# Attention with decay counted within chunks, its products pinned in groups of one tiling, and a weight's two halves added on VectorE

## The chip, the cores and the metric

The kernel runs on one core of a Trainium2 chip. The metric is the time of one execution in microseconds on the device, as the median of a few runs. Five engines work side by side, each on its own queue: TensorE (PE, with its weight loads shown as PEld), VectorE (DVE), ScalarE (ACT), GpSimd (POOL) and SyncE (SP), which issues the transfers here.

## What is computed

Three steps, in float32, on 4 batches of 8 heads with 576 places and 64 columns a head:

```python
scores = q @ k.T / sqrt(64)
D = where(rel >= 0, gamma[h] ** rel, 0)       # rel = query place - key place
x = (scores * D) @ v                          # 2304 tokens x 512
h = x @ w_in                                  # 512 -> 2048
x2 = (h * clip(h + 3, 0, 6) / 6) @ w_out      # 2048 -> 512
h2 = x2 @ w_in2                               # 512 -> 1024
out = layernorm(h2 * softmax(h2)) * g @ w_out2
```

The weights come as float64. `gamma` is 1 - 2^(-5-h) for head h.

## The kernel before

**The order of the work.** Attention comes first, in 16 pairs of heads; the first MLP takes tokens in five blocks (four of 512, one of 256) and its 2048 hidden units in two parts (6 and 10 tiles of 128); the second MLP ends the kernel. Products of the MLPs run as three passes on an exact split of each operand into a rounded high part and a low rest. The units of MLP work are cut into generators of three TensorE products, and the main loop over `attention()` draws some of them between the steps of attention. A scheduler then orders each engine's instructions by its own forecast, except those that `tc.keep_in_program_order` pins. Before the change no TensorE instruction is pinned.

**Attention** (L269 to L412 of the listing below). A chunk is 128 places; there are four, and a fifth of 64. `scores` makes keys x queries for each chunk and both heads (tile `s`, L326), multiplies them on VectorE by a mask of ones and zeros (`st`, L330), then the last chunk's scores (`z`, L341) and each chunk's key-value sum (L346) in the same bank. The state of a chunk is the sum over the chunks before: ScalarE copies the first (L355), VectorE adds the others (L357), both head by head into a 128x128 tile whose other half is zero. `values` multiplies v by `st` (`xp`, L369), then adds state times queries (L377) for both heads in one 128x128 product. The decay gamma^(i-j) is split about the middle place of the sequence: v is multiplied by its half on VectorE in `prep` (L314), x by the other half when it leaves (`evac_x`, L386), with four tables of 576 columns that are loaded from DRAM (`load_tab`).

**Weights** (`split`, L113 to L140). A float64 half tile of 128x512 becomes float32 in this chain: ScalarE scales the upper words (`wz`, L120), VectorE rebuilds exponent and sign (L123 to L126, the last one the lower word), GpSimd adds the two (`wt`, L129), ScalarE rounds the sum to the high part (L131) and VectorE, at each third step GpSimd, makes the rest (L133). There are 48 such steps: 12 during attention, 20 for the first MLP's second part, 16 for the second MLP, whose results go to DRAM. The raw words have two buffers, so the load of one step waits for L126 of the step two before.

**MLP.** `mlp_h` makes h (L190), ScalarE `r` (L200), VectorE `gf` (L201), ScalarE and GpSimd its two parts `g` (L204, L205); `mlp_x2` makes x2 (L211). GpSimd also makes the low part of x (`xb`, L181).

**Where the work meets.** In the loop over `attention()` a pair gives eight steps; weight steps are drawn at every second step from 14 on, MLP units from step 60 on, one and two in turn.

Of the kernel before, what the change touches and what calls it, by code (L numbers as in the profile page):

```python
# [25 lines left out]
MID = S // 2  # L26
# [9 lines left out]
A_FROM = 60  # L36
A_MORE = 2
W_LOAD = 4
W_FROM = 14
W_EVERY = 2  # L40
# [19 lines left out]
def retention_hardswish_solu_kernel(ctx, tc, kt, qt, kn, vt, w1, w2i, w2o, gln, tab, vtab, out):  # L60
    """The products of the two MLPs run as three float32r passes: an operand x is split exactly into
    hi = float32r(x) and lo = x - hi, and x*y = hi*hi + hi*lo + lo*hi. Those of the attention are float32."""
# [26 lines left out]
    # ---------------------------------------------------------------- weights  # L89
    class Weights:  # L90
        """Fills [hi, lo] of half tiles of weights, one at a step, with loads two steps ahead."""
# [21 lines left out]
        def split(self, raw, w, scale=None, done=None):  # L113
            """float32(w) from the words of a float64 w: t takes the upper word (sign, exponent, 20
            bits), z the lower one times the power of two, and their sum is rounded to nearest."""
# [13 lines left out]
            ge.tensor_tensor(out=f, in0=f, in1=z, op=ALU.add)  # L129
# [42 lines left out]
    # ---------------------------------------------------------------- first MLP  # L172
# [10 lines left out]
    def mlp_h(t, ff, g, slot):  # L183
        """h of 128 hidden units, in units of three matmuls, and their part of g."""
# [28 lines left out]
    def mlp(t, ffs, slot, evac):  # L213
        """All of h, then x2 128 columns at a time."""
# [12 lines left out]
    def mlp_by_ff(t, ffs, slot, evac, ps, then=iter(()), n_then=0, ahead=0):  # L227
        """x2 of a short block grows by 128 hidden units at a time, so their weights come free early.
        The last units alternate with those of the work that follows."""
# [9 lines left out]
        for k in range(len(ffs) + X2_LAG):  # L239
            h = mlp_h(t, ffs[k], g, slot) if k <= last else iter(())  # L240
            j = k - X2_LAG
            for d in range(NP):
# [3 lines left out]
                if j >= 0:  # L246
                    # those that share a bank are one group
# [18 lines left out]
    # ---------------------------------------------------------------- attention  # L266
    # A chunk of 128 queries sees the keys of its own chunk through the masked scores and the keys before
# [13 lines left out]
    def load_tab(p):  # L281
        tc.keep_in_program_order(nc.sync.dma_start(out=tab_sb[p], in_=tab[:, p]))
# [429 lines left out]
```

## Time and profile before

| | |
|---|---|
| time, median of 3 runs | 735.05 us (730.48 to 737.5) |
| span of the profiled execution | 733.9 us |
| PE busy in it | 706.9 us, 96%, 3840 products |
| DVE, ACT, POOL busy | 450.5, 293.6, 314.6 us |
| mean granted TensorE clock | 0.962 |

The page gives no time for the profiled execution but its span; the median of the runs lies 1.15 us above that. In the tables of the profile a row of a group gives line, engine, operation, output and inputs, tile, shape and count, then busy time and mean nanoseconds of one, then the idle time ahead of the group and what ended it. Busy time counts overlapping instructions once, so it is not count times mean for TensorE. A timeline row gives start, length, engine, line and count, and in brackets the wait before it. Float32 products of the attention are two instructions each in the trace, those of the MLPs one.

### The profile page before, as it was taken

How to read it: one execution, taken by the hardware profiler on the slowest of the kernel's cores; microseconds unless marked ns; L12 is line 12 of the kernel's file. 1: busy time of each engine (PE TensorE's matmuls, PEld its weight loads, DVE VectorE, ACT ScalarE, POOL GpSimd, SP SyncE). 2: the span in 40 equal slices, each digit the busy share in tenths (PEclk: the TensorE clock that was granted, in tenths of full speed). 3: DMA queues.
4: the chain of work that ended last, by engine and by line, in shares of the span. 5: the costliest groups of instructions: out<-in, count | busy, mean ns of one | idle time of the engine just before them, and what ended most of it. 6: DMA issues, size and time to landing. Idle time of an engine off the chain costs nothing.

```text
span 733.9 us, 10280 instructions
## 1 busy us (share of the span) xinstructions
PE 706.9 (96%) x3840; PEld 576.3 (79%) x3840; DVE 450.5 (61%) x691; ACT 293.6 (40%) x500; POOL 314.6 (43%) x266
## 2 busy tenths in 40 slices
PE   7898989999998999969999999999999999999998
PEld 5677767777887797848878888889988888888887
DVE  3899973432289277772686784511168877776780
ACT  1324421331354354442543532512236654454453
POOL 1445651241266347573583562622235724322333
PEclk7689869999999999989999999999999999999999
DMA  8666644320343342414458457110854733333233
GB/s 323 228 209 225 203 138 163 110 90 29 72 142 117 82 149 87 142 39 125 157 181 281 164 193 238 58 29 29 314 192 114 152 90 77 67 72 85 60 73 86
DMA packets 76834, 98.87 MB, mean 135 GB/s; under 512 B 42864, under 2 KB 45168, under 8 KB 75760
## 3 DMA queue, kind: packets, MB, share of 16 engines
q1 hardware_dynamic: 76784, 98.22, 43.6%
q8 instruction: 30, 0.49, 0.3%
q14 instruction: 20, 0.16, 0.1%
HBM read 64.64 MB, written 24.12 MB: 121 GB/s over the span
## 4 chain that ended last, share of the span: by engine, by line
PE 66%; DVE 11%; issue 8%; DMA 6%; POOL 4%; ACT 3%; SPq 1%; POOLq 0%; DVEq 0%; ACTq 0%
PE h L190 15%; PE o L617 13%; PE h L551 13%; PE x L211 13%; PE acc L211 4%; DMA wraw<-in_w_dram 3%; PE s L326 3%; DVE wt L124 2%; DVE wt L123 2%; PE xp L369 2%; PE xp L377 2%; POOL g L205 2%; DVE wz L126 2%; DVE w L133 1%; DVE gf L201 1%
## 5 line engine op out<-in xcount | busy, mean ns | idle before, releaser
L211 PE MATMUL x<-g,w 128*128 128x512 f32 x648 | 158.0, 399 | 3.6 <-DVE gf L201 2.4
L205 POOL TENSOR_TENSOR g<-gf,g 128x512 fp32r<-128x512 f32 (+1 forms) x80 | 102.6, 1284 | 136.0 <-ACT g L204 134.3
L190 PE MATMUL h<-xb,w 128*128 128x512 f32 (+1 forms) x600 | 139.5, 368 | 9.8 <-ACT w L131 4.8
L211 PEld LDWEIGHTS x<-g,w 128*128 128x128 f32 x648 | 121.2, 190 | 31.8 <-DVE gf L201 3.1
L190 PEld LDWEIGHTS h<-xb,w 128*128 128x128 f32 x600 | 101.7, 193 | 28.4 <-ACT w L131 5.3
L551 PE MATMUL h<-w2i,x2b 128*128 128x512 f32 x432 | 102.0, 389 | 0.0
L617 PE MATMUL o<-w2o,lt 128*128 128x512 f32 (+1 forms) x456 | 101.0, 378 | 0.0
L201 DVE SCALAR_TENSOR_TENSOR gf<-r,h 128x512 f32<-128x512 f32 (+1 forms) x80 | 50.3, 630 | 79.6 <-ACT r L200 62.7
L129 POOL TENSOR_TENSOR wt<-wt,wz 128x512 f32<-128x512 f32 x48 | 67.7, 1411 | 65.3 <-DVE wz L126 65.3
L617 PEld LDWEIGHTS o<-w2o,lt 128*128 128x128 f32 x456 | 82.5, 188 | 16.0
L551 PEld LDWEIGHTS h<-w2i,x2b 128*128 128x128 f32 x432 | 80.6, 188 | 16.3
L181 POOL TENSOR_TENSOR lt<-lT,lt 128x512 fp32r<-128x512 f32 x36 | 46.3, 1306 | 93.9 <-ACT lt L180 93.9
L190 PE MATMUL h<-xB,w 128*128 128x512 f32 x360 | 82.4, 389 | 0.0
L190 PEld LDWEIGHTS h<-xB,w 128*128 128x128 f32 x360 | 67.6, 188 | 14.0
L200 ACT ACTIVATE r<-h,half 128x512 f32<-128x512 f32 (+1 forms) x80 | 50.9, 639 | 57.7 <-PE h L190 57.3
L204 ACT ACTIVATE g<-gf 128x512 fp32r<-128x512 f32 (+1 forms) x80 | 46.9, 588 | 61.9 <-DVE gf L201 61.8
L211 PE MATMUL acc<-g,w 128*128 128x256 f32 (+1 forms) x312 | 63.9, 329 | 1.2 <-POOL g L205 1.1
L123 DVE TENSOR_SCALAR wt<-wz 128x512 int32<-128x512 int32 x48 | 38.3, 801 | 31.5 <-ACT wz L120 31.0
L181 POOL TENSOR_TENSOR xb<-xa,xb 128x512 fp32r<-128x512 f32 (+7 forms) x32 | 29.0, 923 | 66.9 <-ACT xb L180 66.9
L211 PEld LDWEIGHTS acc<-g,w 128*128 128x128 f32 x312 | 50.7, 192 | 8.6 <-POOL g L205 2.1
L124 DVE SCALAR_TENSOR_TENSOR wt<-wz,wt 128x512 int32<-128x512 int32 x48 | 44.9, 937 | 1.1
L126 DVE SCALAR_TENSOR_TENSOR wz<-wraw,wz 128x512 f32<-128x512 uint32 x48 | 42.8, 894 | 1.1
(76 smaller groups left out, 765.8 us busy)
## 6 DMA issues: line engine op xcount, KB each, us to landing
wraw<-in_w_dram SPq DMA_DIRECT2D x32, 512.0 KB, 4.0
rv<-in_vt_dram SPq DMA_DIRECT2D x16, 320.0 KB, 3.9
x2l<-x2s SPq DMA_DIRECT2D x18, 256.0 KB, 4.5
out_dram<-osb SPq DMA_DIRECT2D x17, 256.0 KB, 2.0
x2s<-x2p SPq DMA_DIRECT2D x16, 256.0 KB, 3.5
wraw<-in_w2i_dram SPq DMA_DIRECT2D x8, 512.0 KB, 5.2
w2is<-wsi SPq DMA_DIRECT2D x8, 512.0 KB, 5.1
wraw<-in_w2o_dram SPq DMA_DIRECT2D x8, 512.0 KB, 4.2
```

Source lines behind the costliest of these rows:

```text
L123: ve.tensor_scalar(out=t, in0=zi, scalar1=3, scalar2=None, op0=ALU.logical_shift_left)
L124: ve.scalar_tensor_tensor(out=t, in0=zi, scalar=-2 ** 31, in1=t, op0=ALU.bitwise_and, op1=ALU.bitwise_or)
L126: ve.scalar_tensor_tensor(out=z, in0=raw[:, :, 0].bitcast(U32), scalar=2.0 ** -52, in1=z, op0=ALU.mult, op1=ALU.mult)
L129: ge.tensor_tensor(out=f, in0=f, in1=z, op=ALU.add)
L181: ge.tensor_tensor(out=x[:, 1, c], in0=src, in1=f32(x[:, 0, c]), op=ALU.subtract)
L190: nc.tensor.matmul(hp, w1t[ff][:, a, c], xb[t, p][:, b, :n], start=(p == 0 and i == 0), stop=(p == NP - 1 and i == 2),)
L200: se.activation(out=r, in_=hp, func=ACTF.Relu, scale=1.0 / 6.0, bias=half)
L201: ve.scalar_tensor_tensor(out=gf, in0=r, scalar=1.0, in1=hp, op0=ALU.min, op1=ALU.mult)
L205: ge.tensor_tensor(out=g[ff][:, 1], in0=gf, in1=f32(g[ff][:, 0]), op=ALU.subtract)
L211: nc.tensor.matmul(acc, w1t[ff][:, a, c], g[:, b], start=(first and i == 0), stop=(last and i == 2))
L551: nc.tensor.matmul(h[:, m], x[:, a, c], w[:, b, m * 512:(m + 1) * 512], start=(d == 0 and j == 0), stop=(d == NP - 1 and j == 2),)
L617: nc.tensor.matmul(op, lt[:, a, ff % 4], w[:, b, c:c + n], start=(ff == 0 and j == 0), stop=(ff == NFF2 - 1 and j == 2),)
```

## The change

It has three parts.

**Decay within chunks.** The decay is now counted from the start of each chunk, so all chunks share one table. `prep` multiplies v by gamma^-place, a number per partition, with two ScalarE operations. The mask holds gamma^-128 instead of ones, per pair of heads; x is multiplied by gamma^(place+128) as before, with tables that ScalarE copies from one small loaded array (20 copies ahead of everything else it does). The state now decays from chunk to chunk, state = gamma^128 * state + chunk's sum, both heads at once on 64 columns: one copy and three VectorE operations in place of two and six. The products with the state are two of 64x64 tiles per chunk instead of one of 128x128 on a tile padded with zeros.

**TensorE's order.** All products of attention are pinned, and stand in groups: scores; chunk states and values of the pair before (128x64 tiles); last chunk's scores, its values and the products with the state (64x64 tiles). The chunk sums and last scores have banks of their own, scores have one buffer instead of two. A pair gives three steps. Weight steps are drawn at two of three steps from 5 on, MLP units, two each step, from pair 5 on.

**The add.** In `split` the sum of a weight's two parts is on VectorE.

```diff
-A_FROM = 60
-A_MORE = 2
-W_FROM = 14
-W_EVERY = 2
+W_FROM = 5
+A_FROM = 5
@@ split
-            ge.tensor_tensor(out=f, in0=f, in1=z, op=ALU.add)
+            ve.tensor_tensor(out=f, in0=f, in1=z, op=ALU.add)
@@ attention
+    def mm_a(*args, **kw):
+        tc.keep_in_program_order(nc.tensor.matmul(*args, **kw))
...
-        ve.tensor_tensor(
-            out=v.rearrange("p h c d -> p (h c) d"), in0=rv,
-            in1=vtab_sb[:, pr % NP].unsqueeze(2).to_broadcast([128, 2 * NV, D]), op=ALU.mult,
-        )
+        for h in range(2):
+            head = 128 * NP + 2 * (pr % NP) + h
+            se.activation(
+                out=v[:, h].rearrange("p c d -> p (c d)"),
+                in_=rv[:, NV * h:NV * h + NV].rearrange("p c d -> p (c d)"),
+                func=ACTF.Copy, scale=decay_sb[:, head:head + 1],
+            )
...
+    def chunk_states(pr):
+        rn, v = raws[pr][2], vs[pr]
+        up = ps_a.tile([128, 4, 64], F32, tag="u", bufs=1, name=f"u{pr}")
+        state = states[pr] = pa.tile([128, 4, 64], F32, tag="state", bufs=2, name=f"state{pr}")
+        for c in range(4):
+            for h in range(2):
+                mm_a(up[HEADS[h], c], rn[:, c, HEADS[h]], v[:, h, c], start=(c == 0), stop=(c == 3))
+        at = 128 * NP + H + pr % NP
+        se.activation(out=state[:, 0], in_=up[:, 0], func=ACTF.Copy)
+        for c in range(1, 4):
+            ve.scalar_tensor_tensor(
+                out=state[:, c], in0=state[:, c - 1], scalar=decay_sb[:, at:at + 1], in1=up[:, c],
+                op0=ALU.mult, op1=ALU.add,
+            )
...
+    def from_states(pr):
...
+        for h in range(2):
+            mm_a(xp[HEADS[h], at_x(4)], v[HEADS[h], h, 4], st4[HEADS[h]], start=False, stop=False)
-            nc.tensor.matmul(xp[:, to], state[:, c - 1], rq[:, CHUNKS[c]], start=False, stop=(c == 4))
+            for h in range(2):
+                mm_a(
+                    xp[HEADS[h], at_x(c)], state[HEADS[h], c - 1], rq[HEADS[h], CHUNKS[c]],
+                    start=False, stop=(c == 4),
+                )
...
     def attention():
+        for pr in range(NPAIR + 1):
+            if pr < NPAIR:
+                scores(pr)
+                yield pr
+                prep(pr + 1)
+                if pr + 2 >= EARLY:
+                    load_pair(pr + 2)
+                chunk_states(pr)
+            if pr:
+                values(pr - 1)
+            yield pr
+            if pr < NPAIR:
+                last_scores(pr)
+            if pr:
+                from_states(pr - 1)
+            yield pr
...
+    for p in range(NP):
+        for c in CHUNKS:
+            se.activation(out=tab_sb[p][:, c], in_=decay_sb[:, 128 * p:128 * p + c.stop - c.start], func=ACTF.Copy)
...
-        if s >= W_FROM and (s - W_FROM) % W_EVERY == 0:
+        if s >= W_FROM and (s - W_FROM) % 3 != 2:
             wq.step()
-        if s >= A_FROM:
-            for _ in range(1 + (s % A_MORE == 0)):
+        if pr >= A_FROM:
+            for _ in range(2):
                 next(mlp_a, None)
```

Three places show how instructions move. On TensorE, in the middle of attention, before (s_ are scores, z_ the last chunk's scores and the chunks' sums, xp_ the values with st_ and state_, x_ products of the MLP):

```order
L326 MATMUL s_1058<-rq_867,rk_866 128x128 x2
L211 MATMUL x_0_0_1050<-g_3_957,w_3_150 128x512 x3
L326 MATMUL s_1058<-rq_867,rk_866 128x128
L211 MATMUL x_0_0_1050<-g_4_983,w_4_151 128x512
L326 MATMUL s_1058<-rq_867,rk_866 128x128 x3
L211 MATMUL x_0_1_1093<-g_3_957,w_3_150 128x512 x3
L211 MATMUL x_0_1_1093<-g_4_983,w_4_151 128x512
L326 MATMUL s_1058<-rq_867,rk_866 128x128
```

The same place with the change (L286 is the helper that pins every product of attention, u_ are the chunks' sums):

```order
L286 MATMUL s_1037<-rq_860,rk_859 128x128 x8
L210 MATMUL x_0_0_1047<-g_0_658,w_0_176 128x512 x3
L210 MATMUL x_0_0_1047<-g_1_737,w_1_177 128x512 x3
L286 MATMUL u_1065<-v_958,rn_861 64x64 x8
L286 MATMUL xp_1079<-st_934,v_856 64x128 x8
L210 MATMUL x_0_0_1047<-g_2_825,w_2_178 128x512 x3
L210 MATMUL x_0_0_1047<-g_3_900,w_3_179 128x512 x3
L286 MATMUL z_1094<-rq_860,rk_859 64x64 x2
L286 MATMUL xp_1079<-st_1000,v_856 64x64 x2
L286 MATMUL xp_1079<-rq_744,state_970 64x128 x6
L286 MATMUL xp_1079<-rq_744,state_970 64x64 x2
```

A pair's eight score products stand in one piece, with six MLP products before each next group.

On TensorE again, from pair 2's last scores on, before (h_ are products of the MLP):

```order
L341 MATMUL z_342<-raw_130 64x64 x2
L346 MATMUL z_342<-v_208,raw_130 64x64 x8
L190 MATMUL h_0_799<-xb_0_226,w_0_147 128x512 x3
L190 MATMUL h_0_799<-xb_1_319,w_0_147 128x512
L326 MATMUL s_376<-rq_215,rk_214 128x128 x2
```

With the change, from pair 4's scores to the first MLP products behind pair 5's:

```order
L286 MATMUL s_491<-rq_329,rk_328 128x128 x8
L286 MATMUL u_524<-v_419,rn_330 64x64 x8
L286 MATMUL xp_538<-st_396,v_325 64x128 x8
L286 MATMUL z_547<-rq_329,rk_328 64x64 x2
L286 MATMUL xp_538<-st_454,v_325 64x64 x2
L286 MATMUL xp_538<-rq_230,state_431 64x128 x6
L286 MATMUL xp_538<-rq_230,state_431 64x64 x2
L286 MATMUL s_585<-rq_423,rk_422 128x128 x8
L189 MATMUL h_0_607<-xb_0_281,w_0_176 128x512 x3
```

The first MLP product moves from behind pair 2 to behind the scores of pair 5.

On VectorE, in the weight steps of the first MLP's second part, before (wt and wz are the two parts, w the weight's rest, gf a factor of the MLP):

```order
L126 SCALAR_TENSOR_TENSOR wz<-wraw,wz 128x512
L133 TENSOR_TENSOR w_7_1957<-wt,w_7_1957 128x512
L123 TENSOR_SCALAR wt<-wz 128x512
L201 SCALAR_TENSOR_TENSOR gf_1_2022<-r_1_2021,h_1_1996 128x512
L124 SCALAR_TENSOR_TENSOR wt<-wz,wt 128x512
```

With the change (lines are one less):

```order
L125 SCALAR_TENSOR_TENSOR wz<-wraw,wz 128x512
L122 TENSOR_SCALAR wt<-wz 128x512
L128 TENSOR_TENSOR wt<-wt,wz 128x512
L123 SCALAR_TENSOR_TENSOR wt<-wz,wt 128x512
L200 SCALAR_TENSOR_TENSOR gf_1_2097<-r_1_2096,h_1_2071 128x512
```

The add stands one operation behind its input on the same engine, and the next step's first operation is between them.

More of the change, by code (lines that the diff above doesn't have):

```diff
@@ L25 @@
 FA = 6
-MID = S // 2
+GAMMA = [1.0 - 2.0 ** (-5 - h) for h in range(H)]
+N_DEC = 128 * (H // 2) + H + H // 2
 NPAIR = NH // 2
@@ L59, in retention_hardswish_solu_kernel @@
 @with_exitstack
[L60 removed]
+def retention_hardswish_solu_kernel(ctx, tc, kt, qt, kn, vt, w1, w2i, w2o, gln, decay, out):
     nc = tc.nc
@@ L270, in retention_hardswish_solu_kernel, with at_x @@
     ps_a = tc.alloc_tile_pool(name="ps_a", bufs=1, space=bass.MemoryType.PSUM)
+    decay_sb = pa.tile([128, N_DEC], F32, name="decay_sb")
     tab_sb = [pa.tile([128, S], F32, name=f"tab_sb{p}") for p in range(NP)]
-    vtab_sb = pa.tile([128, NP, 2 * NV], F32, name="vtab_sb")
-    mask = pa.tile([128, 4, 128], F32, name="mask")
-    mask4 = pa.tile([128, 64], F32, name="mask4")
-    state_bd = [pa.tile([128, 4, 128], F32, name=f"state{i}") for i in range(2)]
-    raws, vs, sts, states = {}, {}, {}, {}
+    mask = pa.tile([128, NP, 2, 128], F32, name="mask")
+    mask4 = pa.tile([128, NP, 64], F32, name="mask4")
+    raws, vs, sts, sts4, states, us, xps = {}, {}, {}, {}, {}, {}, {}
     HEADS = [slice(0, 64), slice(64, 128)]
     CHUNKS = [slice(128 * c, min(128 * c + 128, S)) for c in range(NV)]
-    def load_tab(p):
-        tc.keep_in_program_order(nc.sync.dma_start(out=tab_sb[p], in_=tab[:, p]))
+    def at_x(c):
+        return slice(384 + CHUNKS[c].start, 384 + CHUNKS[c].stop)
+    def mm_a(*args, **kw):
+        tc.keep_in_program_order(nc.tensor.matmul(*args, **kw))
     def load_pair(pr):
@@ L298, in load_pair @@
         if pr == 0:
-            nc.sync.dma_start(out=vtab_sb, in_=vtab)
+            nc.sync.dma_start(out=decay_sb, in_=decay)
         if early:
@@ L336, in scores @@
-        v = vs[pr]
-        sp = ps_a.tile([128, 2, 512], F32, tag="s", bufs=2, name=f"z{pr}")
-        st4 = sts[pr, 4] = pa.tile([128, 64], F32, tag="st4", bufs=2, name=f"st4{pr}")
-        state = states[pr] = state_bd[pr % 2]
-        for h in range(2):
-            nc.tensor.matmul(
-                sp[HEADS[h], 0, :64], k[HEADS[h], CHUNKS[4]], q[HEADS[h], CHUNKS[4]], start=True, stop=False
-            )
+                mm_a(sp[:, h, CHUNKS[c]], k[HEADS[h], CHUNKS[c]], q[HEADS[h], CHUNKS[c]], start=(c == 0), stop=(c == 3))
@@ L358, in scores @@
-        yield
-    def values(pr):
-        xp = ps_a.tile([128, 1024], F32, tag="xp", bufs=1, name=f"xp{pr}")
-        rq, v, state, st = raws.pop(pr)[1], vs.pop(pr), states.pop(pr), sts.pop(pr)
-        st4 = sts.pop((pr, 4))
-        for c in range(NV):
-            to = slice(384 + CHUNKS[c].start, 384 + CHUNKS[c].stop)
+                mm_a(xp[HEADS[h], at_x(c)], v[:, h, c], st[:, h, CHUNKS[c]], start=(c <= 1), stop=(c == 0))
+    def from_states(pr):
+        xp = xps.pop(pr)
+        rq, v, state, st4 = raws.pop(pr)[1], vs.pop(pr), states.pop(pr), sts4.pop(pr)
+        for h in range(2):
+            mm_a(xp[HEADS[h], at_x(4)], v[HEADS[h], h, 4], st4[HEADS[h]], start=False, stop=False)
+        for c in range(1, NV):
```

97 lines of the change are left out of this document (34 added, 63 removed).

## The prediction

> **What bounds the kernel now.** The busy table by stretch came first. Each row gives the stretch, then busy time and instructions of PE, PEld, DVE, ACT and POOL, TensorE's granted clock, DMA share and GB/s.
>
> ```profile
> 4.80:112.00 107.20, 96.76 (x749) 74.01 (x748) 88.20 (x163) 34.82 (x75) 48.40 (x40) 0.78 0.65 219
> 112.00:190.50 78.50, 78.50 (x583) 59.42 (x581) 28.72 (x65) 20.66 (x45) 17.15 (x18) 1.00 0.34 105
> 232.00:246.00 14.00, 11.51 (x47) 8.76 (x48) 10.16 (x13) 6.81 (x12) 8.16 (x8) 1.00 0.05 20
> 311.00:332.00 21.00, 14.84 (x52) 10.85 (x51) 13.82 (x15) 8.61 (x15) 14.83 (x11) 0.84 0.16 50
> 332.00:395.00 63.00, 61.73 (x271) 50.47 (x270) 37.49 (x46) 23.88 (x40) 35.52 (x25) 1.00 0.55 176
> 395.00:734.00 339.00, 335.65 (x1617) 283.56 (x1615) 201.89 (x292) 150.72 (x228) 131.59 (x116) 1.00 0.42 121
> ```
>
> TensorE is the bound almost everywhere; VectorE shares it until 112 us. From 395 us on nothing but TensorE's own work shows, and the change doesn't touch it. What can move is a front up to 112 us with the clock at 0.78, an attention stage to 190.5 us where TensorE never rests, and holes around 240, 320 and 377 us.
>
> The clock is read from 4 us slices, with the wait ahead of them from TensorE's timeline.
>
> ```profile
> 96.65 0.33 PE L341 MATMUL z<-rq,rk 64*64 64x64 f32 x2 [1.80 <-DVE st L330]
> ...
> 108.00:112.00 4.00, 4.00 (x24) 2.76 (x24) 1.22 (x1) 0.00 (x0) 0.56 (x1) 0.57 0.00 0
> ```
>
> After a wait of 1.80 us, ended at 96.65, the clock is still near half in the slice before 112 us, though TensorE is busy throughout: some 13 us, of which half is lost. [...]
>
> **Part 1, TensorE's attention work.** One pair of heads without interruption, at full clock, and pieces of an interrupted one:
>
> ```profile
> 43.76 1.16 PE L326 MATMUL s<-rq,rk 64*128 64x128 f32 x16
> 44.86 1.35 PE L369 MATMUL xp<-st,v 128*64 128x128 f32 x20
> 46.14 1.10 PE L377 MATMUL xp<-rq,state 128*128 128x128 f32 x8
> 47.18 0.33 PE L341 MATMUL z<-rq,rk 64*64 64x64 f32 x4
> 47.44 0.69 PE L346 MATMUL z<-v,rn 128*64 128x64 f32 x16
> 48.05 1.16 PE L326 MATMUL s<-rq,rk 64*128 64x128 f32 x16
> ...
> 137.86 0.49 PE L326 MATMUL s<-rq,rk 64*128 64x128 f32 x4
> 138.28 0.97 PE L190 MATMUL h<-xb,w 128*128 128x512 f32 x3
> ```
>
> From 43.76 to 48.05 is 4.29 us. A score group takes 1.10 us whole, but 0.42 us a quarter (137.86 to 138.28): four quarters are 1.68, so a break, which a burst of MLP products makes, costs about 0.2. An MLP product itself is 0.227 us: in a long run 24 take 5.44.
>
> ```profile
> 599.78 5.44 PE o L617 x24
> ...
> L211 PE MATMUL x<-g,w 128*128 128x512 f32 x114 | 30.1, 405 | 0.0
> L190 PE MATMUL h<-xb,w 128*128 128x512 f32 x87 | 23.2, 406 | 0.0
> L326 PE MATMUL s<-rq,rk 64*128 64x128 f32 x80 | 9.0, 312 | 0.0
> L377 PE MATMUL xp<-rq,state 128*128 128x128 f32 (+1 forms) x56 | 8.3, 279 | 0.0
> ```
>
> These groups are of 112 to 190.5 us: 201 MLP products are 45.6 us, and the other 32.9 go to 5 pairs by the scores (80/16), 7 by the states (56/8), so 6: **5.5 us a pair**.
>
> Now the order shows scores, six MLP products, chunk states with values, six, all 64x64 products, six. The chunk states and values share one tiling, and so do the last scores, their values and the products with the states. The latter become 8 pairs of 64x64 tiles instead of 4 full ones: as many columns if the two heads run side by side. The z row, two heads in such tiles, takes 0.26 us, little over the fixed start, so I take side by side; one after the other they'd cost 3.5 x 128 columns again, 0.75 us (three quarters of the 1.04 between the L377 row and the next). A pair then costs 4.29, less 0.3 for three tiling changes fewer, plus 3 x 0.2: **4.6 us** (bounds 4.3 and 5.3). Over the some ten pairs with MLP work among them that is 9 us.
>
> **Part 2, the front.** VectorE is full there. Groups of 20 to 106 us:
>
> ```profile
> 20.00:106.00 86.00, 78.20 (x618) 60.22 (x617) 79.71 (x148) 31.38 (x68) 45.24 (x38) 0.82 0.63 206
> ...
> L357 DVE TENSOR_TENSOR state<-z,state 64x64 f32<-64x64 f32 x54 | 11.9, 221 | 3.1 <-ACT state L355 1.6
> L126 DVE SCALAR_TENSOR_TENSOR wz<-wraw,wz 128x512 f32<-128x512 uint32 x12 | 11.8, 984 | 0.2
> L124 DVE SCALAR_TENSOR_TENSOR wt<-wz,wt 128x512 int32<-128x512 int32 x12 | 9.8, 821 | 0.2
> L330 DVE TENSOR_TENSOR st<-s,mask 128x1024 f32<-128x1024 f32 x8 | 9.7, 1216 | 0.1
> L123 DVE TENSOR_SCALAR wt<-wz 128x512 int32<-128x512 int32 x12 | 7.7, 652 | 0.3 <-ACT wz L120 0.2
> L133 DVE TENSOR_TENSOR w<-wt,w 128x512 fp32r<-128x512 f32 x8 | 7.5, 942 | 1.9 <-ACT w L131 1.8
> L314 DVE TENSOR_TENSOR v<-rv,vtab_sb 128x640 f32<-128x640 f32 x8 | 7.4, 920 | 0.1
> L125 DVE TENSOR_SCALAR wz<-wt 128x512 int32<-128x512 int32 x12 | 7.0, 587 | 0.1
> L386 DVE TENSOR_TENSOR xa<-xp,tab_sb 128x576 f32<-128x576 f32 x8 | 6.0, 751 | 0.1
> ```
>
> Per pair VectorE did 1.22 + 6 x 0.22 + 0.92 + 0.75 and a small mask product (0.2): 4.4 us. Now v is on ScalarE, which is busy 31 of 86 us, and three 64-column updates (0.25 each) replace six: 2.9 us. A weight step cost 0.65 + 0.82 + 0.59 + 0.98 + two thirds of 0.94: 3.7 us. The add joins it, and GpSimd's add leaves:
>
> ```profile
> 234.45 0.42 DVE L123 TENSOR_SCALAR wt<-wz 128x512 int32<-128x512 int32 x1
> 234.90 1.66 DVE L124 SCALAR_TENSOR_TENSOR wt<-wz,wt 128x512 int32<-128x512 int32 x1
> ...
> 234.67 1.33 POOL L129 TENSOR_TENSOR wt<-wt,wz 128x512 f32<-128x512 f32 x1 [2.36 <-DVE wz L126]
> ```
>
> The L124 operation ends when GpSimd's add ends, at 1.66 us against its mean of 0.82: an add holds VectorE up by about 0.8. Its price on VectorE lies between 0.68 (half of the 1.33) and 0.94, the L133 mean, which is the nearest row, also two inputs of this size; I take 0.8, so a step stays near 3.8. [...]
>
> But the order moves steps and MLP work. Steps start after pair 1, two per pair, and no MLP product stands ahead of pair 5's scores. From some 20 us, when the first weights have landed (they stay behind pair 3's loads on SP's queue), to pair 8's scores VectorE has 12 steps (46 us), 6 pairs more (18), five products gf (3.4) and some 4 us of gaps, as before: 91 us. TensorE there has 54 MLP products and eight pairs, some 49 us at full clock: it waits, partly at half clock. Before, pair 8's scores began here, with so many products done:
>
> ```profile
> 81.88 1.16 PE L326 MATMUL s<-rq,rk 64*128 64x128 f32 x16
> ...
> L190 PE MATMUL h<-xb,w 128*128 128x512 f32 x67 | 20.1, 442 | 2.7 <-ACT xb L180 2.0 <-ACT w L131 0.7
> ```
>
> That is 82 us and 67 products, so the front **loses 9 + 13 x 0.227 = 12 us**. At the start, 16 copies for the decay table precede v of pair 0 on ScalarE, 0.3 us each by the 128-column row:
>
> ```profile
> L180 ACT ACTIVATE xb<-xa 128x128 fp32r<-128x128 f32 x4 | 1.2, 298 | 0.3 <-PE h L190 0.3
> ```
>
> That is 5 us; TensorE waited for the second pair's loads in that time anyway, so I count 1 us, in the 20 above. The four tables of 288 KB that leave SP's queue return about as much.
>
> From there TensorE bounds: 8 pairs at 4.6 and 216 products at 0.227 are 86 us, 177 in all, with 1.5 us for a wait: 178.5 when attention and 270 products are done. Before, attention ended at 190.5 with 303 products; less 33 x 0.227, that is 183. The two parts together **gain 4.5 us** (bounds: a gain of 16 if the front loses nothing, a loss of 16 by (b) below).
>
> **Part 3, the later weight steps.** The holes sum to 2.5 (14.00 - 11.51), 6.2 and 1.3 us in the rows above, and half clock in the second costs 0.16 x 21 = 3.4: 13 us. The largest:
>
> ```profile
> 322.79 1.04 PE L190 MATMUL h<-xb,w 128*128 128x512 f32 x2 [4.07 <-ACT w L131]
> ...
> 318.97 1.71 POOL L205 TENSOR_TENSOR g<-gf,g 128x512 fp32r<-128x512 f32 x1 [3.55 <-ACT g L204]
> 320.64 1.44 POOL L129 TENSOR_TENSOR wt<-wt,wz 128x512 f32<-128x512 f32 x1
> ```
>
> The weight's add stands behind a g on GpSimd, and TensorE waits for ScalarE's copy of that sum. On VectorE it would follow its input directly and end 2 us or more earlier, and g no longer stands behind adds. Late next is the load: a buffer comes free only after L126. I take two thirds, **8.5 us**, between 0 (loads decide) and 13. Beyond 395 us the adds lengthen VectorE's 202 of 339 us; TensorE covers it, and without that cover the second MLP's 16 steps at 0.8 would be 13 us.
>
> **Sum.** 733.9 - 4.5 - 8.5 = 720.9. This is against the profiled execution's span; the median of the runs, 735.05, lies 1.15 above it, so **722 us**.
>
> **Rivals.** (a) The two heads' 64x64 tiles write one bank and take turns: 16 x 0.75 = 12 us, **734**. For it: the new products of a pair share a bank, which the scores' don't. Against: the z row, also in one bank, at 0.26. (b) Slower: TensorE, pinned and without MLP work to slip in, stays at half clock until pair 8. From pair 5 to 8 it has 54 products (12.2) and three pairs (13.8), 26 us, which become 52; VectorE has 5.5 steps (21), three pairs (9), four gf (2.7) and gaps, 35. So 17 us more, and the 6 us of a last rewarming, of which the sum has 1.5: **743**. This decides if the waits of pairs 2 to 5 hold the clock at 0.5 through pair 7. For it: the 1.80 us wait. Against: TensorE would then be busy all the time, and the clock rose after 13 us of that. (c) The later holes stay, because loads and a longer VectorE queue take GpSimd's place: **730.5**. Part of the change that doesn't do what it says would be this one.
>
> **Chances.** Forecast 0.55, (a) 0.12, (b) 0.15, (c) 0.18. A measurement of this kernel can tell about 1% from no change. Faster by over that (below 727.7) takes the forecast and a little of (c), 0.58; within 1% 0.27; slower, (b), 0.15. The range is 706 (735 less 16 and 13, the bounds of the two gains) to 741, between (a) and (b), where most of (b) is left out; the forecast's own is 708 to 729.
>
> **What would show it.** Right: scores of a pair unbroken at 1.1 us, products with the states near 1 us, attention ending near 178 us; L123 to L126 of the old numbering below 0.75 us in mean; no wait of 4 us for weights near 310 us. Wrong: the 64x64 group near 2 us; the clock at 0.5 beyond 80 us; pair 8's scores after 100 us; the wait for weights as long as before.

## The result and the profile after the change

The changed kernel takes 716.2 us (median of four runs, 715.16 to 717.43) where the kernel before takes 736.27 us (730.48 to 738.67) beside it. The ratio is 0.974, 95% interval 0.969 to 0.979: 2.6% faster. The forecast was 722 us, range 706 to 741. The profiled execution took 715.41 us, with a span of 713.7 us against 733.9: 20.2 us less, where the sum had 13.0.

To see where they went one needs a point of the program that both traces show. The first products of the fourth block's h will do; ahead of them the rows count 374 MLP products (216 and 158 by line) in both. The columns are start, duration of the group, what it does, how many products. First the timeline of TensorE before, then after:

```profile
206.75 2.43 PE L190 MATMUL h<-xb,w 128*128 128x512 f32 x10
```

```profile
192.06 2.43 PE L189 MATMUL h<-xb,w 128*128 128x512 f32 x10
```

So 14.7 us come from attention and the front (forecast 4.5). Behind this point 527.15 us became 521.64, 5.5 us (forecast 8.5). The first stretch of the busy table, with the columns as in the prediction:

```profile
4.80:112.00 107.20, 86.15 (x924) 67.58 (x924) 81.78 (x143) 46.84 (x114) 33.38 (x32) 0.87 0.71 234
```

Up to 112 us TensorE is busy for 10.6 us less than before (86.15 against 96.76) and does more (120 MLP products against 102): the clock is 0.87 instead of 0.78 and the groups are whole. VectorE, which the change relieves of v and three of six state sums a pair and loads with the add, has 82 us of work there instead of 88.

Pair 9 of the attention on TensorE's timeline:

```profile
89.51 1.16 PE L286 MATMUL s<-rq,rk 64*128 64x128 f32 x16
90.60 1.66 PE L210 MATMUL x<-g,w 128*128 128x512 f32 x6
...
93.69 1.66 PE L210 MATMUL x<-g,w 128*128 128x512 f32 x6
...
95.56 0.94 PE L286 MATMUL xp<-rq,state 64*64 64x128 f32 x16
96.42 1.66 PE L210 MATMUL x<-g,w 128*128 128x512 f32 x6
98.01 1.16 PE L286 MATMUL s<-rq,rk 64*128 64x128 f32 x16
```

From 89.51 to 98.01 is 8.50 us, of which 18 MLP products at 0.227 are 4.09: a pair costs 4.4 us, where it was 5.5. The scores take 1.09 us to the next start, unbroken. The products with the states in 64x64 tiles take 0.86 (95.56 to 96.42), where the same columns in 128x128 tiles took 1.04, so the two heads run side by side.

VectorE's groups between 20 and 96 us show what a weight step costs now:

```profile
L123 DVE SCALAR_TENSOR_TENSOR wt<-wz,wt 128x512 int32<-128x512 int32 x12 | 10.2, 849 | 0.3
L128 DVE TENSOR_TENSOR wt<-wt,wz 128x512 f32<-128x512 f32 x12 | 10.1, 842 | 0.1
L125 DVE SCALAR_TENSOR_TENSOR wz<-wraw,wz 128x512 f32<-128x512 uint32 x12 | 9.0, 753 | 0.1
L122 DVE TENSOR_SCALAR wt<-wz 128x512 int32<-128x512 int32 x11 | 8.6, 779 | 1.5 <-ACT wz L119 1.2
L132 DVE TENSOR_TENSOR w<-wt,w 128x512 fp32r<-128x512 f32 x8 | 6.1, 760 | 1.4 <-ACT w L130 1.3
L124 DVE TENSOR_SCALAR wz<-wt 128x512 int32<-128x512 int32 x12 | 5.0, 417 | 0.1
```

And the wait for the last weight of the second set, which was 4.07 us:

```profile
304.61 1.11 PE L189 MATMUL h<-xb,w 128*128 128x512 f32 x2 [2.38 <-ACT w L130]
```

### The profile page after: what moved, and what is told of

It is laid out like the page before. It is cut to its first block, busy times and chain, and to the rows that moved or that the text cites. A ratio compares the mean times of both kernels' runs of the same rounds, so it can differ in the third digit from the quotient of the medians.

```text
span 713.7 us, 10518 instructions
## 1 busy us (share of the span) xinstructions
PE 680.6 (95%) x3968; PEld 560.5 (79%) x3968; DVE 441.9 (62%) x673; ACT 307.2 (43%) x536; POOL 249.1 (35%) x233
## 4 chain that ended last, share of the span: by engine, by line
PE 70%; DVE 12%; DMA 7%; issue 5%; ACT 3%; POOL 1%; SPq 0%; DVEq 0%; POOLq 0%; ACTq 0%
PE h L189 17%; PE x L210 16%; PE o L625 14%; PE h L559 14%; DMA wraw<-in_w_dram 6%; PE acc L210 4%; PE xp L286 3%; DVE wt L122 2%; DVE wt L123 2%; DVE wz L125 2%; ACT wz L119 1%; DVE wt L128 1%; PE s L286 1%; DVE wz L124 1%; PE u L286 1%
## 5 line engine op out<-in xcount | busy, mean ns | idle before, releaser
L210 PE MATMUL x<-g,w 128*128 128x512 f32 x648 | 154.6, 393 | 3.0 <-DVE gf L200 1.5
L189 PE MATMUL h<-xb,w 128*128 128x512 f32 (+1 forms) x600 | 137.3, 366 | 3.9 <-ACT w L130 2.4
L122 DVE TENSOR_SCALAR wt<-wz 128x512 int32<-128x512 int32 x48 | 33.4, 695 | 39.4 <-ACT wz L119 39.0
L128 DVE TENSOR_TENSOR wt<-wt,wz 128x512 f32<-128x512 f32 x48 | 44.8, 934 | 0.6
L119 ACT ACTIVATE wz<-wraw 128x512 f32<-128x512 f32 x48 | 31.5, 662 | 26.7 <-DMA wraw<-in_w_dram 21.4
L130 ACT ACTIVATE w<-wt 128x512 fp32r<-128x512 f32 x32 | 20.2, 631 | 45.0 <-DVE wt L128 45.0
```

The costliest lines, as they stand in the source:

```text
L119: first = se.activation(out=z, in_=raw[:, :, 1].bitcast(F32), func=ACTF.Copy, scale=2.0 ** -112)
L122: ve.tensor_scalar(out=t, in0=zi, scalar1=3, scalar2=None, op0=ALU.logical_shift_left)
L128: ve.tensor_tensor(out=f, in0=f, in1=z, op=ALU.add)
L189: nc.tensor.matmul(hp, w1t[ff][:, a, c], xb[t, p][:, b, :n], start=(p == 0 and i == 0), stop=(p == NP - 1 and i == 2),)
L210: nc.tensor.matmul(acc, w1t[ff][:, a, c], g[:, b], start=(first and i == 0), stop=(last and i == 2))
```

## The experiments

My theory after reading the trace: attention's order and the add are two separate gains; in the front VectorE sets the pace, so that neither the clock nor ScalarE's v matters there; from pair 9 on TensorE does, and there whole groups count.

### The two parts apart

The add back on GpSimd, the rest as changed:

```diff
-            ve.tensor_tensor(out=f, in0=f, in1=z, op=ALU.add)
+            ge.tensor_tensor(out=f, in0=f, in1=z, op=ALU.add)
```

> The changed kernel with one line undone: the sum of a weight's two parts is on GpSimd again. My theory: the add's move is worth what lies behind the first product of the fourth block, 5.5 us (527.2 us from there to the end before, 521.6 after), and little ahead of it, since an add on GpSimd holds VectorE up by about as much as it costs there. So 716 + 5.5 = 721 to 724 us, the first product of the fourth block still near 192 us, and the wait for the last weight of the second set, 2.4 us after the change, back at 4 us with half a clock behind it. Rival 1: the later gain comes from the attention's end being earlier or from chance, and the add is worth nothing: under 718 us. Rival 2: the front hangs on it too, because ScalarE's copy of a weight waits for the sum and the next pair's v stands behind that copy: over 726 us, with the fourth block's first product after 197 us.

The kernel before with the same line edited the other way:

> The kernel before with nothing but the sum of a weight's two parts on VectorE. My theory: the later holes give 5 us, and in the front VectorE, which is its bound, gets 0.7 us more work a step but isn't held up by GpSimd's add any more: about even. So some 730 us against 735 (ratio 0.993), the first product of the fourth block at 205 to 208 us as before. Rival 1: worth nothing, 735 us. Rival 2: VectorE in the front is overloaded by 12 steps of 0.7 us, and the fourth block begins 5 to 8 us later: 736 to 738 us in all. Rival 3: the front gains as well, 725 us or less, and the attention's new order has little part in the whole gain.

Measured: 723.13 us with the add back (ratio to the kernel before 0.983, 0.980 to 0.987), 727.11 us with the add alone (0.990, 0.986 to 0.994), 736.41 us before. Attention alone is worth 13.3 us, the add alone 9.3, which adds up to 22.6; both together are worth 20.1 (20.2 by the spans): nearly additive. My theory of the first run holds; the add by itself was worth more than the 5 us expected of it. The fourth block's first products and the wait for the last weight with the add back:

```profile
193.31 2.43 PE L189 MATMUL h<-xb,w 128*128 128x512 f32 x10
...
310.89 0.81 PE L189 MATMUL h<-xb,w 128*128 128x512 f32 x2 [3.94 <-ACT w L130]
```

The 193.31 is 1.25 us later than with the add on VectorE, and the rest of the span, 528.8 us, is 7.2 longer. The hole is back at 3.94 us. VectorE between 20 and 96 us in the same run:

```profile
L123 DVE SCALAR_TENSOR_TENSOR wt<-wz,wt 128x512 int32<-128x512 int32 x12 | 11.3, 943 | 0.3
L125 DVE SCALAR_TENSOR_TENSOR wz<-wraw,wz 128x512 f32<-128x512 uint32 x12 | 9.1, 761 | 0.1
...
L124 DVE TENSOR_SCALAR wz<-wt 128x512 int32<-128x512 int32 x12 | 8.3, 694 | 0.1
L122 DVE TENSOR_SCALAR wt<-wz 128x512 int32<-128x512 int32 x12 | 6.9, 574 | 8.2 <-ACT wz L119 8.2
L132 DVE TENSOR_TENSOR w<-wt,w 128x512 fp32r<-128x512 f32 x8 | 6.1, 765 | 5.3 <-ACT w L130 5.3
```

A step is 943 + 761 + 694 + 574 + two thirds of 765 ns, 3.48 us, against 4.15 with the add. VectorE saves 0.67 us a step, yet the front isn't shorter: it stands idle for 8.2 and 5.3 us, waiting for ScalarE's z and w. Both stand on ScalarE's queue, which waits in ten places, 26.5 us in all, for the step's sum, 1.37 us each on GpSimd (its mean there); the z itself waits for loads alone, 3.1 us. In the front, then, the add's move trades VectorE's idle time for work.

With the add alone, the fourth block begins at 204.14 us, 2.6 us earlier than before; the expectation had it even. That execution took 730.24 us, near the slowest of its six, and behind this point it is 2.9 us shorter than the kernel before. It isn't the old order with one operation moved: the scheduler, which places products that aren't pinned, set TensorE's differently too (the scores at 101.67 and 109.45 us stand in one piece, where the kernel before has pieces).

### The order of TensorE's products

The products of the attention not pinned:

```diff
-        tc.keep_in_program_order(nc.tensor.matmul(*args, **kw))
+        nc.tensor.matmul(*args, **kw)
```

> The changed kernel with the attention's products not pinned: the scheduler may place MLP products among them. The order that comes out keeps scores and values whole up to pair 8, and later lets whole MLP tiles run ahead of a pair. My theory: whole groups are what counts, and these stay whole by the way the code is written, so the pin itself is worth 0 to 3 us: 716 to 719 us. Rival: the pin is what holds the front in step, and without it MLP products that wait for their weights stand ahead of ready scores: 722 us or more, with waits for weights on TensorE ahead of 112 us.

716.94 us (713.78 to 718.3), first products of the fourth block at 192.11: the pin is worth nothing that can be measured. The trace shows the groups still whole up to 125 us, by the way the code is written.

The groups broken into pieces, everything still pinned:

```diff
+    def part_of_mlp(pr):
+        if pr >= A_FROM:
+            next(mlp_a, None)
...
                 mm_a(sp[:, h, CHUNKS[c]], k[HEADS[h], CHUNKS[c]], ...)
+            if c < 3:
+                part_of_mlp(pr)
...
                 mm_a(xp[HEADS[h], at_x(c)], v[:, h, c], st[:, h, CHUNKS[c]], ...)
+            if c == 1:
+                part_of_mlp(pr + 1)
...
                     start=False, stop=(c == 4),
                 )
+            if c == 2:
+                part_of_mlp(pr + 1)
...
-        if pr >= A_FROM:
-            for _ in range(2):
-                next(mlp_a, None)
+        if pr >= A_FROM and s % 3 == 2:
+            next(mlp_a, None)
```

> The changed kernel with the same products and pins, but the six bursts of MLP products that go with a pair are of three products each and stand inside the groups: three within the scores, one within the values, one within the products with the states, one at the pair's end (instead of three bursts of six between groups). My theory: a break costs 0.2 us. Five breaks more and two bursts less between groups, 0.6 to 1.0 us a pair over the 11 pairs that have MLP work with them, is 7 to 11 us; and the clock, which after a short wait comes back in 3.5 to 5 us where groups are whole, stays at half for 8 to 13 us where they are broken, as it did in the kernel before: up to 6 us more. Together 723 to 733 us. Rival 1: the front up to pair 8 is set by VectorE and hides the breaks there, and the clock does not care for the order: about seven pairs at 0.8, 720 to 722 us, half clock no longer than 5 us. Rival 2: breaks cost nothing, 716 us.

721.86 us, 5.7 more than the changed kernel and 4.9 more than the run before, measured beside it: the first rival, not my theory. Pair 9 in that run:

```profile
87.94 0.49 PE L286 MATMUL s<-rq,rk 64*128 64x128 f32 x4
88.37 0.96 PE L210 MATMUL x<-g,w 128*128 128x512 f32 x3
89.26 0.49 PE L286 MATMUL s<-rq,rk 64*128 64x128 f32 x4
...
97.95 0.49 PE L286 MATMUL s<-rq,rk 64*128 64x128 f32 x4
```

Pair 10 begins at 97.95, where whole groups had it at 98.01, with 90 MLP products done in both: until then VectorE hides the breaks. From there a pair with its 18 products takes 10.0 us instead of 8.5, and the fourth block's first products come at 197.16, 5.1 us later. A quarter of the scores is 0.43 us to the next start, as the forecast's row had it; what the forecast left out is that a burst of three MLP products takes 0.89 us (88.37 to 89.26) and not 3 x 0.227 = 0.68. A break costs on both sides of the switch: 0.2 us in the group that it breaks, and 0.1 more for a burst of three than for half a burst of six (1.59). The clock, against my theory, stays at 1.00 from 50 to 112 us in this run; its longest waits there, 1.04 us (ended at 50.95) and 1.33 us (ended at 56.70), did not drop it, so this run can't tell how long a low clock lasts with broken groups.

### What sets the pace of the front

Four runs change one thing each: v back on VectorE, a third buffer for v, fillers that keep the clock up, and less of a weight step on VectorE.

```diff
-            se.activation(out=v[:, h]..., in_=rv[:, NV * h:NV * h + NV]..., func=ACTF.Copy, scale=...)
+            ve.tensor_scalar(out=v[:, h]..., in0=rv[:, NV * h:NV * h + NV]..., scalar1=..., op0=ALU.mult)
```

> The changed kernel with v times its decay on VectorE again, as two operations with a factor for each row (128x320 each), not on ScalarE. My theory: VectorE sets the pace of the front, so 0.6 to 0.9 us more a pair for the eight pairs up to 77 us move everything behind them: 5 to 7 us, 721 to 723 us, with pair 8's scores at 82 to 84 us instead of 76.9. Rival 1: what counts is TensorE's waits for ScalarE's v, 12.1 us in six places; these go, and the kernel gains 3 us or more: under 714 us. Rival 2: the two cancel, 715 to 718 us.

719.08 us, 2.9 more than the changed kernel and 3.6 more than the next run, measured beside it, with pair 8's scores at 81.84 and the fourth block at 195.62, 3.6 us later: my theory's sign, some half its size. TensorE's waits for ScalarE, 12.1 us after the change, fell to 4.8, which may be the other half; no run shows it.

```diff
-        v = vs[pr] = pa.tile([128, 2, NV, D], F32, tag="v", bufs=2, name=f"v{pr}")
+        v = vs[pr] = pa.tile([128, 2, NV, D], F32, tag="v", bufs=3, name=f"v{pr}")
```

> The changed kernel with three buffers for v instead of two, so that v of a pair can be made a pair earlier and doesn't wait for the last products of the pair before. My theory: VectorE, busy 31.1 of 33 us from 44 to 77 us, sets the front; TensorE's 12.1 us of waits for v turn into waits for VectorE's st and xa, and at most the first pairs gain: 713 to 716 us. Rival: these waits and the half clock behind them are the bound; without them the front is 6 to 10 us shorter, 706 to 710 us, pair 8's scores before 70 us.

715.48 us: nothing. What TensorE waits for between 5 and 112 us (in all, times, longest), first in the changed kernel, then with three buffers:

```profile
PE u L286 <- ACT v L320: 12.1, 6, 3.9
PE s L286 <- DVE st L334: 4.7, 3, 1.8
PE xp L286 <- DVE xa L387: 4.1, 5, 1.9
```

```profile
PE xp L286 <- DVE xa L387: 9.0, 5, 2.5
PE u L286 <- ACT v L320: 7.2, 3, 3.7
PE s L286 <- DVE st L334: 5.6, 3, 2.6
```

The sums are 20.9 and 21.8 us. Waits for v became waits for VectorE's xa: v was the last to arrive, not what sets the pace.

```diff
+    def fill(pr, n):
+        for _ in range(n if 1 <= pr < A_FROM else 0):
+            mm_a(warm, ones[:, :128], ones[:, 128:], start=True, stop=True)
...
+                fill(pr, 6)
                 scores(pr)
+                fill(pr, 8)
                 yield pr
...
+    ones = pa.tile([128, 640], mybir.dt.bfloat16, name="ones")
+    ve.memset(ones, 0.0)
```

> The changed kernel with bfloat16 products that nobody reads pinned into TensorE's waits of pairs 1 to 4 (six ahead of a pair's scores, eight behind them, some 0.2 us each at full clock), so that the clock has no reason to fall there. My theory: the clock stays at 1.0 from 14 to 44 us, yet the front is set by VectorE and the time changes by 1 us or less: 715 to 717 us. Rival 1: half clock is the cost; three stretches of 3.5 to 5 us of it go, 2 us each, 5 to 7 us in all: 709 to 711 us. Rival 2: the fillers stand in the way of ready products and cost up to 1 us a pair: 718 to 720 us.

From 20 to 44 us in the busy table (the changed kernel has TensorE busy for 14.14 us there, at a clock of 0.72):

```profile
20.00:44.00 24.00, 21.77 (x281) 14.93 (x282) 21.17 (x37) 11.33 (x25) 7.08 (x7) 1.00 0.62 198
```

The clock is at 1.00, TensorE looks busy, and pair 5's scores begin at 43.42 instead of 43.75, the fourth block at 192.27 instead of 192.06. Half clock there, up to pair 5, costs nothing. The whole took 713.92 us (713.18 to 715.94), 2.3 less than the changed kernel; that lies behind the fourth block, where the edit changes nothing, and its ratio (0.970, 0.965 to 0.976) overlaps that of the changed kernel, so I don't count it as a better version.

```diff
-                eng = ge if self.at % 3 == 2 else ve
+                eng = ge if self.at % 3 == 2 or self.pin and self.at % 3 == 1 else ve
```

> The changed kernel with two of three low parts of the first set's weights (and of the second MLP's first weights, which nothing waits for) made on GpSimd instead of one of three: in the front VectorE has four subtractions less, 0.76 us each. My theory that VectorE sets the front's pace: 3 us less there if nothing else changes, 712 to 714 us. Against it stands that a subtraction of two inputs on GpSimd (1.36 us) holds up VectorE's own two-input operations: L123's mean rises from 0.85 us, and the gain is then 0 to 1 us, 715 to 717 us. Rival: TensorE comes to wait for GpSimd's part of the weights, 718 us or more.

717.96 us, 1.8 more, where my theory had 712 to 714: no gain. Its ratio (0.978, 0.972 to 0.984) overlaps that of the changed kernel, so a loss isn't shown. The time is close to the rival's, but not by its mechanism, for up to 112 us TensorE waits nowhere for GpSimd's part. Of VectorE's groups from 20 to 90 us the one that changed most:

```profile
L124 DVE TENSOR_SCALAR wz<-wt 128x512 int32<-128x512 int32 x12 | 8.0, 664 | 0.3
```

Four subtractions fewer save 3.4 us on VectorE (6.1 to 2.7), and L123, L124, L125 and L128 take 3.5 us more together (34.3 to 37.8), of which L124 alone 3.0: three of its twelve take 1.25 to 1.40 us, each beside an operation of GpSimd (at 30.57 and 54.22 a subtraction), and eight 0.41 to 0.43. Here work moved from VectorE to GpSimd came back in full.

### How long the clock stays low

The granted clock, read in steps of 0.25 us, falls and rises on one grid. In the changed kernel the low stretches begin at 7.75, 24.75, 35.0, 62.25, 82.75 and 304.75 us. Counted as 87 periods, the 297.0 us from the first to the last make one of 3.414 us; the others lie 4.98, 7.98, 15.96 and 21.97 of these behind the first. They last 7, 7, 7, 3.75, 3.75 and 3.5 us. In the kernel before they last 13.75, 13.75, 7, 13.75 and 7 us: four or two periods. The periods around the wait at 96.65 us in the kernel before:

```profile
94.43:97.85 3.42, 1.56 (x11) 1.04 (x12) 3.33 (x7) 0.63 (x1) 2.16 (x2) 0.99 0.42 147
97.85:101.26 3.41, 3.41 (x25) 2.83 (x26) 3.29 (x8) 1.20 (x2) 1.27 (x1) 0.50 0.34 100
...
108.09:111.50 3.41, 3.41 (x16) 2.34 (x18) 0.81 (x1) 0.00 (x0) 0.47 (x1) 0.51 0.00 0
111.50:114.91 3.41, 3.41 (x43) 2.60 (x40) 2.00 (x3) 0.67 (x2) 0.07 (x1) 1.00 0.21 68
```

And around pair 8's waits after the change:

```profile
79.53:82.94 3.41, 1.14 (x23) 0.92 (x24) 3.26 (x9) 2.51 (x6) 0.00 (x0) 0.99 0.98 308
82.94:86.36 3.42, 3.42 (x19) 2.70 (x16) 3.33 (x4) 1.91 (x5) 2.58 (x2) 0.51 0.76 244
```

The periods in which TensorE is busy for 1.56 (94.43 to 97.85) and 1.14 us (79.53 to 82.94) of 3.41 are each followed by one at half clock. Up to 112 us half clock follows nine periods at full clock in the two traces, with 0.96 to 1.60 us of work; behind one of 1.58 us (55.64 to 59.05 after the change) the clock stayed at 0.99, and behind those of 2.03 us or more at 0.99 or 1.00. So the 45% (1.53 us) of an expectation below is near what was seen, but no sharp line. After the change one busy period (82.94 to 86.36) brings the clock back; in the kernel before four were needed, though the records show TensorE busy in all of them.

Two pairs of runs were to tell whether the order makes the difference, by a wait put in where TensorE otherwise never rests. In all four the MLP products of pairs 10 to 12 are pinned as well; the broken ones start from the kernel with broken groups, and the number of repeats differs (nine in place of six here, eight in place of nine in the second pair).

```diff
-        for h in range(2):
+        for h in (0, 1) * (6 if pr == 11 else 1):
```

> A measurement of the clock. The changed kernel, in which v of pair 11 is computed six times over (some 1 us each on ScalarE, the same values), so that TensorE stands before pair 11's chunk states at about 110 us, where it otherwise never waits; the MLP products of pairs 10 to 12 are pinned too, so that none slips into the wait. Ahead of it and behind it the groups are whole, with bursts of six MLP products between them. ScalarE's 6 us less the 2.75 us until the states' turn is a wait of some 3 us. My theory: the clock falls to half and is back within 3.5 to 5 us, as it was in the front after this change. Rival: the length of half clock depends on where in some period of the clock's own the wait falls, not on the order of the products; then it can be anything from 3.5 to 13 us here as well. The whole kernel 717 to 722 us.

> The counterpart: the kernel with broken groups (bursts of three MLP products inside scores, values and products with the states), v of pair 11 computed nine times (9 us, less the 5.2 us until the states' turn in this order), the MLP products of pairs 10 to 12 pinned: again a wait of some 3 us at about 110 us. My theory: the changes of tiling and the small pieces keep TensorE from counting as fully busy, and the clock stays at half for 8 to 13 us, as in the kernel before after its 1.80 us wait. Rival: back within 5 us as with whole groups; then the long half clock in the kernel before has another cause. The whole kernel 724 to 732 us.

The waits came out shorter than meant, and unequal. With whole groups 1.35 us, ended at 111.47, did not drop the clock at all. With broken ones 2.01 us, ended at 115.28, did, for two periods (114.75 to 121.75), less than my theory's 8 us. 720.02 and 728.6 us in one run each. Since the waits differ, this pair says nothing on the order. So the wait was moved ahead of the scores and made longer:

```diff
-        ve.tensor_tensor(out=st..., in0=sp..., in1=mask..., op=ALU.mult)
+        for _ in range(9 if pr == 10 else 1):
+            ve.tensor_tensor(out=st..., in0=sp..., in1=mask..., op=ALU.mult)
```

> The clock again, with the wait ahead of the scores and long enough to be sure of a fall. In all runs up to now the low clock lies on one grid of 3.41 us (after the change its stretches begin at 7.85 us and whole multiples of that behind it, and last one or two periods; in the kernel before, four, two and four): a period in which TensorE works less than some 45% drops the clock for the next ones, and it comes back at the end of a period with enough work. The question is what makes it four periods. Here: the changed kernel with the masked copy of pair 10's scores made nine times on VectorE (the same values), so that pair 11's scores wait some 5 us near 110 us; MLP products of pairs 10 to 12 pinned; groups whole. My theory: one or two periods of half clock behind the wait, 3.4 to 6.8 us. Rival (the order doesn't matter): as many as in the counterpart with broken groups. The whole kernel 720 to 726 us.

> The counterpart with broken groups: the masked copy of pair 10's scores made eight times, pair 11's scores, in four pieces with three MLP products behind each of the first three, wait some 5 us near 112 us. My theory: scores in pieces between MLP products, as behind the wait at 96.65 us in the kernel before, do not let a period count as busy though the records show TensorE busy, so the clock stays at half at least until the pieces are through, about 10 us at half clock: three or four periods, 10 to 14 us. Rival: one or two periods, as with whole groups; then the four periods in the kernel before have a cause that neither order explains. The whole kernel 727 to 736 us.

722.21 and 730.29 us in one run each, with waits of 5.01 us (ended at 111.10) and 5.56 us (ended at 114.47). The periods with whole groups, and then with broken ones:

```profile
109.25:112.66 3.41, 1.56 (x14) 1.59 (x16) 1.71 (x2) 0.00 (x0) 0.00 (x0) 0.52 0.04 16
112.66:116.07 3.41, 3.41 (x14) 2.15 (x13) 1.23 (x1) 0.00 (x0) 0.00 (x0) 0.50 0.00 0
116.07:119.49 3.42, 3.42 (x48) 2.69 (x50) 0.84 (x3) 0.22 (x1) 0.00 (x0) 0.98 0.21 77
```

```profile
111.06:114.47 3.41, 0.00 (x0) 0.03 (x1) 3.24 (x3) 0.00 (x0) 0.58 (x2) 0.50 0.28 100
114.47:117.88 3.41, 3.41 (x12) 2.21 (x13) 0.00 (x0) 0.00 (x0) 0.00 (x0) 0.50 0.00 0
117.88:121.30 3.42, 3.42 (x10) 1.79 (x9) 0.00 (x0) 0.00 (x0) 0.00 (x0) 0.51 0.00 0
121.30:124.71 3.41, 3.41 (x52) 2.50 (x53) 2.01 (x5) 0.22 (x1) 0.00 (x0) 1.00 0.28 77
```

Whole groups: one busy period (112.66 to 116.07) and the clock is back. Broken groups: the first busy period (114.47 to 117.88), a quarter of the scores (two products, four instructions) and three products of the MLP in turn, was not enough; the second, of the same kind, was. The direction is my theory's, the size is one period, not the two or three more of the kernel before. That the order can cost a period is seen in this one pair.

The other traces bear on it too. Take the periods at half clock, on each trace's own grid, that the records show busy for at least 3.3 of 3.41 us. In the changed kernel and the eleven runs made from it there are 46, and full clock followed on all but one, the first busy one with broken groups above. In the kernel before and the run with the add alone there are 23, and 13 were followed by half clock again. Bursts of MLP products aren't what these share: in the kernel before, two of them lie ahead of its first MLP product (26.59 us), where scores and products with the states take turns in pieces of two to six instructions:

```profile
12.51:15.93 3.42, 3.42 (x18) 2.64 (x16) 2.16 (x7) 0.91 (x3) 0.00 (x0) 0.50 1.05 397
15.93:19.34 3.41, 3.41 (x31) 2.77 (x30) 1.96 (x2) 0.78 (x2) 0.69 (x1) 0.50 1.02 391
```

So slow returns go with the old kernel's order of products. What in it makes them slow, and four periods long, stays open.

## Why the prediction was right, and where its steps were off

The verdict was as forecast, and two of its three mechanisms were: unbroken groups make a pair cheaper, and with the add on VectorE the later wait for weights shrinks. The third, the front's loss, was not. The measured 716 lies in the forecast's own range of 708 to 729, yet one step of the sum is off by 14 us and two by 3 to 4 the other way: that they partly cancel is luck. Of the signs named for being right, attention's end came 10 us before its 178, and of the four means that were to be below 0.75 us only L124's clearly is (0.42; L125 has 0.753, L122 0.78, L123 0.85); the others came true. Attention's end with 270 MLP products, forecast at 178.5 us and at 183 before, came at 168.4. Pair 8's scores, with 54 products, began at 76.9, before at 78.9 by the same count (81.88 less 13 products). By the steps of the sum, with the gain in the profiled executions:

| step | forecast | measured |
|---|---|---|
| up to pair 8's scores, at equal products | loses 12 | gains 2.0 |
| from there to attention's end, at equal products | gains 16.5 | gains 12.6 |
| both | 4.5 | 14.6 |
| later weight steps and the rest | 8.5 | 5.5 |

- **A pair at 4.6 us** (bounds 4.3 to 5.3): right, 4.4. Eight pairs at 1.1 less are 8.6 of the 12.6 us. No run shows the 0.3 us for three changes of tiling alone, only the pair as a whole. The start that a short group pays is seen in the kernel before: two instructions of 64 columns take 0.25 us to the next start (54.76 to 55.01), four 0.26 (53.58 to 53.84).
- **The front loses 12 us**: this is the step that failed. It put all twelve weight steps of VectorE ahead of pair 8's scores, at 91 us. VectorE's total was right; what was wrong is who waits for it. After the change, first on TensorE, then on VectorE:

```profile
76.89 1.16 PE L286 MATMUL s<-rq,rk 64*128 64x128 f32 x16
...
81.38 0.69 PE L286 MATMUL u<-v,rn 128*64 128x64 f32 x16 [1.74 <-ACT v L320]
82.60 1.74 PE L286 MATMUL xp<-st,v 128*64 128x128 f32 x16 [0.53 <-DVE xa L387]
```

```profile
85.53 1.21 DVE L334 TENSOR_TENSOR st<-s,mask 128x1024 f32<-128x1024 f32 x1
...
88.50 0.68 DVE L128 TENSOR_TENSOR wt<-wt,wz 128x512 f32<-128x512 f32 x1
```

  The twelfth add runs at 88.50, close to the forecast's 91, and pair 8's masked copy (st) at 85.53. But the scores, at 76.89, need only that pair 7's were copied; nine of the twelve adds had begun by then. TensorE ran ahead, 14 us earlier than forecast, and lost 4 of them at once: pair 8 with its 18 products took 12.6 us (76.89 to 89.51), where 8.5 are due. The forecast equated "VectorE gets to pair 8" with "TensorE starts pair 8"; a queue that runs a pair ahead shifts the wait behind it.
- **The add at 0.8 us, a step staying near 3.8**: the price was right (842 ns in the front: ten of twelve take 0.68 or 0.69 us, the two that begin behind an operation of GpSimd 1.68 and 1.58), the sum not: 4.15 us with the add, 3.48 without. GpSimd's add does hold VectorE up, but by less than I took (L123 to L125 gain some 0.38 us, L122 loses 0.2). That it cost nothing is due to the chain through GpSimd, which the run with the add back showed.
- **Half clock at 6 us for a wait** (half of the 13 us behind the wait ended at 96.65; the sum itself has 1.5, which no run shows): mis-sized and misplaced. After the change a wait costs one or two periods, 1.7 or 3.4 us of TensorE's work, and up to pair 5 none of it counts, as the fillers showed. Where it did count is the kernel before: its stretch from 97.85 to 111.50 lies where TensorE is the bound, and costs half of 13.65 us, 6.8, against 1.7 for the stretch from 82.94 to 86.36 after. With the pairs' 8.6, 5.1 for this and 0.5 back for longer waits (2.27 us at pair 8 against 1.80), 13.2 us stand against the measured 12.6. That this stretch is gone is seen; that it goes by the order of the products is only partly shown. In the run with the add alone, with attention's code as before, it is gone too, after a longer one earlier than the kernel before has there (two periods from 73.86 us):

```profile
73.75:84.25 10.50, 9.41 (x52) 7.19 (x51) 10.18 (x20) 3.50 (x8) 3.00 (x4) 0.51 0.65 221
97.75:111.50 13.75, 11.60 (x107) 8.66 (x104) 12.30 (x28) 3.50 (x8) 1.72 (x2) 1.00 0.51 163
```

  No wait of TensorE's from 85 to 111 us is longer than 0.90 us in that run. So these 5.1 us can't be put down to attention's part alone.
- **The later holes, 8.5 us**: the add is worth 7.2 there (528.8 against 521.6). That only 5.5 show is because attention's part alone makes this stretch 1.65 us longer (528.8 against 527.15 before); I haven't found why, and one profile each may not resolve it.
- **Rivals.** (a) The 64x64 tiles taking turns fell with 0.86 us where 2 were due (the prediction's "8 pairs of 64x64 tiles" are eight tiles, four pairs). (b) Half clock up to pair 8 fell: between pair 5's start and pair 8's the clock is low for one period only, from 62.46 us on. (c) The later holes staying fell with the run that has the add back.

## What to carry to other kernels

Where two engines share the pace, list for each start of the one what it really needs of the other, and how many steps the one can run ahead: the amount of work alone (right here to 2.5 us) doesn't give the time. The releaser in the list of waits is the last to arrive, not the cause; an extra buffer for it that changes nothing (12.1 us of waits became 7.2 and 4.9 elsewhere) tells this cheaply. Where TensorE is the bound, keep products of one tiling together, and count a break on both sides of it (here 0.2 us in the group and 0.1 in the burst; the broken groups took 5.7 us more in all). Where another engine was, neither the breaks nor the half clock that were tried here cost anything (pair 10 at 97.95 against 98.01, the fourth block at 192.27 against 192.06).

## What the runs showed of the hardware

- In these traces the clock changes on a fixed grid of 3.41 us. How the wait lies in it matters: in the changed kernel a wait of 2.38 us ended at 304.61, within one period (301.34 to 304.76), and dropped the clock, while in the run with fillers 2.56 us at the same place of the program, ended at 303.57 and cut by a period's end near 302.1 (61 periods behind the end of a low stretch near 93.9), left it at 1.00. That chance alone is worth 1.7 us here.
- A period that the records show as busy throughout may still not bring the clock back (four such from 97.85 to 111.50 in the kernel before, of which the last did; one in the run with broken groups). By the count above, 45 of 46 such periods did in the twelve traces of the changed kernel and its variants, and 10 of 23 in the two with the old order.
- Two-input operations of VectorE that began early in an operation of GpSimd took longer in these traces: after the change ten of twelve L123 take 0.67 to 0.69 us, and two 1.53 and 1.78, at 71.58 and 83.82, where GpSimd's began at 71.23 and 83.78. The add at 28.04, begun 0.10 us ahead of an operation of GpSimd, takes 0.69, and so do the L123 at 30.18 and 41.27, in the last 0.15 us of GpSimd's. L124 with one input took longer too, 0.42 us in the mean after the change and 0.69 with the add back, where three of twelve take 1.37 to 1.54.
